# Two batches of v loaded without a cast, and two more TensorE transposes handed to the DMA, in a fused attention and MLP kernel

## The chip, the cores and the metric

One core of one Trainium2 chip runs the whole program. The metric is device time in microseconds (us). Engines are named as in the profile: PE (TensorE matmul), PEld (its weight load), DVE (VectorE), ACT (ScalarE), POOL (GpSimd), SP (SyncE, which here only issues DMAs).

## The reference

Attention with a relative position bias, eight batches of eight heads, 576 positions, head size 64; then a two-layer MLP with a leaky ReLU on all 4608 tokens. Inputs and output are float32; the kernel computes in bfloat16 with float32 accumulation.

```python
q, k, v: (8, 8, 576, 64)     bias_table: (32, 8)
scores = scale * q @ k.T + bias[bucket(|i - j|)]     # scale = 1/8
attn = softmax(scores);  a = attn @ v                # (8, 8, 576, 64)
x = a.transpose(0, 2, 1, 3).reshape(4608, 512)
h = x @ w_in                                         # (512, 2048)
out = maximum(0.01 * h, h) @ w_out                   # (2048, 512)
```

## The kernel before, in words

**The unit of work** is a pair of heads: `items` lists 32 pairs, n = 0 to 31, four to a batch (`n_pairs` = 4, `b` the batch, `p` the pair in it). For each pair, q and k are turned so that the head size lies on the partitions (`transpose_q`, `transpose_k`, lines 287 to 295), scores are made key by query (`qk_mm`, 297), exponentiated on ACT (`exp`, 322), multiplied by the bias band on DVE (`band`, 334), and multiplied with v (`av_tails`, 352, for the last 64 keys; `av`, 365, for the other 512, once for each head of the pair). `av` ends with a reciprocal and a multiply on DVE (375, 376) into `opair`, bf16. `x_transposes` (382) turns `opair` into `xT`, the MLP's input.

**Two ways to turn.** With TensorE: 12 small transposes for q and 12 for k into PSUM (line 275), five for an output (394), each followed by a copy out of PSUM. By DMA: for q and k, `pair_rows` (252) first copies both heads side by side with two DVE copies (257), then `turn_by_dma` (263) issues one transposing DMA on SP's queue into a tile `tu`, and the copies of lines 290 and 294 read `tu`; for an output, one transposing DMA straight into `xT` (387). `by_dma(n)` (260) sends q and k of pairs n > 8 by DMA, and `x_by_dma(n)` (379) the outputs of n = 6, 8, 9 and on to 30. `turn_ahead` (637) prepares pair n + 2 in pass n for the first few pairs, n + 3 later. Where pair n + 1 goes by DMA, `begin(n)` (632) does this at the start of the pass; otherwise it is done in the loop behind the first `band` (line 734).

**Loads.** All of q, k, v and the weights come over GpSimd's DMA queue (q0 in the profile), which turns float32 into bf16 on the way. q, k and v have two buffers each (`qn`, `kn`, `vn`, `v4`; batch b uses buffer b % 2). GpSimd works its instructions off in order, a load that must wait holds up those behind it, and by the trace it issues a load only when the eighth load before it has landed. `loads(n)` (607) says what is issued in which pass: in pass 0 the first half of `w_in`, all of batch 1's v (four chunks of 128 positions, `load_v_part`, 117, and the 64 that are left, `load_v_tail`, 130), the second half of `w_in`, the first of `w_out`; in pass 2 half of batch 2's q and k and the rest of `w_out`; from batch 1 on, in passes p = 1, 2, 3, the next batch's loads, behind a one-element copy `tick` (621) that waits for an earlier pair's output.

**The MLP** is cut in pieces of four matmuls (`ffn_in`, 411, one of 16 column blocks for a block T of 512 tokens; `ffn_out`, 438). They are woven between the attention's steps by a plan (`plan`, `slot`, `moe_block`), in an order written out by hand; T = 0 begins in pass 4, T = 1 in pass 9. The activated values lie in `gt`, 16 KB a partition, from a pool with two buffers.

**Order of the loop pass** (714 to 782): loads and turning ahead; scores 0 and 1; `av_tails` and first `av` of pair n - 1; then, when pair n + 1 goes by DMA, `band(n, 0)` before `transpose_q(n + 1)`, otherwise after it; an MLP piece; second `av`; `band(n, 1)`; `transpose_k(n + 1)`; an MLP piece; scores 2, 3 and 4; `x_transposes(n - 1)`; the rest. Score 4 (line 305) writes the two PSUM banks that `av`'s outputs held, so it waits for DVE's second multiply.

Of the kernel before, what the change touches and what calls it, by code (L numbers as in the profile page):

```python
# [10 lines left out]
FP32 = mybir.dt.float32  # L11
BF16 = mybir.dt.bfloat16
# [25 lines left out]
def kernel(  # L38
# [10 lines left out]
    nc = tc.nc  # L49

    B, H, S, D = q.shape
# [4 lines left out]
    P = 128  # L56
    n_pairs = H // 2
    NJ = S // P
# [3 lines left out]
    TT = 512  # L62
    n_tt = NT // TT
    n_fc = DF // P
# [11 lines left out]
    gt_pool = ctx.enter_context(tc.tile_pool(name="gt", bufs=2))  # L76
# [17 lines left out]
    NBUF = 2  # L94
# [4 lines left out]
    vn = [per.tile([P, NJ, H, D + 1], BF16, name=f"vn{i}") for i in range(NBUF)]  # L99
# [9 lines left out]
    def load_qk(b, h0, h1):  # L109
        i = b % NBUF  # L110
        for src, dst in ((q, qn[i]), (k, kn[i])):
            nc.gpsimd.dma_start(  # L112
                out=dst[0:RQ, h0:h1, :, :].rearrange("r h c d -> r h (c d)"),
                in_=src[b, h0:h1, :, :].rearrange("h (r c) d -> r h (c d)", c=NC),
            )

    def load_v_part(b, chunks, h0=0, h1=H):
        for c in chunks:
            nc.gpsimd.dma_start(  # L119
                out=vn[b % NBUF][:, c, h0:h1, 0:D],  # L120
                in_=v[b, h0:h1, c * P : (c + 1) * P, :].rearrange("h s d -> s h d"),
            )

    def load_v_head(b, h):
        nc.gpsimd.dma_start(
            out=vn[b % NBUF][:, :, h, 0:D],
            in_=v[b, h, 0 : NJ * P, :].rearrange("(c s) d -> s c d", s=P),
        )

    def load_v_tail(b):  # L130
        for e in range(2):
            nc.gpsimd.dma_start(
                out=v4[b % NBUF][e * SL : (e + 1) * SL, :, 0:D],
                in_=v[b, e::2, NJ * P : S, :].rearrange("h s d -> s h d"),
            )
# [43 lines left out]
    for j, (u, lo, w, m) in enumerate(groups):  # L179
        copy = nc.scalar.copy if j % 3 == 2 else nc.vector.tensor_copy  # L180
        copy(out=ub[:, C0 + lo : C0 + lo + m * w].rearrange("h (m w) -> h m w", w=w),
             in_=e8[:, u : u + m].unsqueeze(2).to_broadcast([H, m, w]))
    row = ub[:, :]
    nc.vector.tensor_copy(
        out=ub[:, C0 - BAND + 1 : C0],
        in_=bass.AP(tensor=row.tensor, offset=row.offset + C0 + BAND - 1,
                    ap=[list(row.ap[0]), [-1, BAND - 1]]),
# [32 lines left out]
    load_qk(0, 4, 6)  # L220
    clear_edges(nc.vector, 1)
    load_v_head(0, 0)
    load_v_head(0, 1)
    load_v_tail(0)
    load_qk(0, 6, H)
# [7 lines left out]
    def load_w_in(half):  # L233
        o = slice(half * (DF // 2), (half + 1) * (DF // 2))
        nc.gpsimd.dma_start(out=w_in_sb[:, :, o], in_=moe_w_in[:, o].rearrange("(c p) f -> p c f", p=P))

    def load_w_out(half):
        n = n_fc // 2
        nc.gpsimd.dma_start(
            out=w_out_sb[:, half * n : (half + 1) * n, :],  # L240
            in_=moe_w_out[half * n * P : (half + 1) * n * P, :].rearrange("(f p) e -> p f e", p=P),
        )
# [4 lines left out]
    N = len(items)  # L247
# [10 lines left out]
                                  in_=src[b % NBUF][0:RQ, 2 * p : 2 * p + 2, :, :].rearrange("r e c d -> r c e d"))  # L258

    def by_dma(n):  # L260
        return n > 2 * n_pairs

    def turn_by_dma(n):
        t = turned[n] = tu_pool.tile([P, 2 * NC, RQ], BF16, name="tu")
# [2 lines left out]
    def turned_pair(n, j):  # L267

        if by_dma(n):
            return turned[n][:, j * NC : (j + 1) * NC, :].rearrange("p c r -> p r c")  # L270
        ps = ps_m_pool.tile([P, 8 * P], BF16, name="ps_t", tag="m")
        b, p = items[n]
        for c in range(NC):
            for e in range(2):
                nc.tensor.transpose(ps[e * D : (e + 1) * D, c * RQ : (c + 1) * RQ],  # L275
                                    in_=(qn, kn)[j][b % NBUF][0:RQ, 2 * p + e, c, :],
                                    identity=ident[0:RQ, 0:RQ])
        return ps[:, 0:S].rearrange("p (c r) -> p r c", c=NC)
# [98 lines left out]
                                in1=rcp.to_broadcast([P, NJ + 1, D]), op=ALU.mult)  # L377

    def x_by_dma(n):
        return n_pairs + 2 <= n < N - 1 and n != 2 * n_pairs - 1  # L380

    def x_transposes(n):
        b, p = items[n]
        opair = ops_[n]
        w = (NJ + 1) * P
        if x_by_dma(n):
            nc.sync.dma_start_transpose(
                out=xT[p][:, b * S : b * S + w].rearrange("p (i t) -> p i t", t=P),
                in_=opair.rearrange("p i d -> p (i d)"),
            )  # L390
            return
        ps = ps_m_pool.tile([P, 8 * P], BF16, name="ps_tx", tag="m")
        for ic in range(NJ + 1):
            nc.tensor.transpose(ps[:, ic * P : (ic + 1) * P], in_=opair[:, ic, :], identity=ident)  # L394
        nc.vector.tensor_copy(out=xT[p][:, b * S : (b + 1) * S], in_=ps[:, 0:S])


    gts = {}
    rest = {"on": False, "turn": 0}

    def bank(name):

        if rest["on"]:
            turn = rest["turn"] = (rest["turn"] + 1) % 6
            if turn % 3 == 0:
                return ps_o_pool.tile([P, 512], FP32, name=name, tag=f"o{turn // 3}")
            if turn % 3 == 1:
                return ps_s_pool.tile([P, 512], FP32, name=name, tag="ps_s")
        return ps_m_pool.tile([P, 512], FP32, name=name, tag="m")

    def ffn_in(T, f, spare=None):
        if f == 0:
            gts[T] = gt_pool.tile([P, n_fc, TT], BF16, name="gt")
        t0 = T * TT
        if spare is None:
            pm = bank("pm1")
        else:
            pm = ps_o_pool.tile([P, 512], FP32, name="pm1", tag=f"o{spare}")
        for c in range(n_cc):
            nc.tensor.matmul(pm, lhsT=w_in_sb[:, c, f * P : (f + 1) * P], rhs=xT[c][:, t0 : t0 + TT],  # L420
                             start=(c == 0), stop=(c == n_cc - 1))
        return pm
# [61 lines left out]
    def step(kind):  # L484
        T, s = made[kind], at_piece[kind]
        at_piece[kind] = (s + 1) % n_fc
        if at_piece[kind] == 0:
            made[kind] += 1
        return T, s
# [5 lines left out]
    def piece_in(spare=None):  # L495
        T, s = step("in")
        leaky(T, s, ffn_in(T, s, spare))
# [51 lines left out]
    def moe_block():  # L549

        done = 0
        while not can("out") and can("in") and done < 4 and room["left"] > 0:
            T, f = step("in")
            leaky(T, f, ffn_in(T, f, 0 if done == 3 and room["left"] > 1 else None), done == 1)
            room["left"] -= 1
            done += 1
            if done < 3:
                yield
        while done < 2:
            done += 1  # L560
            yield
        if room["split"]:
            yield
            piece_out()
            piece_out()
        elif can("out") and room["left"] >= 4:
            for part in range(4):
                piece_out()
                room["left"] -= 1
                if part == 1:  # L570
                    yield
            moe(2, 0 if room["left"] > 1 else None)
        else:
            yield
            moe(2)
        yield
# [30 lines left out]
    def loads(n):  # L607

        b, p = items[n]
        if n == 0:  # L610
            load_w_in(0)
            load_v_part(1, range(NJ))
            load_v_tail(1)
            load_w_in(1)
            load_w_out(0)
        elif n == 2:
            load_qk(2, 0, H // 2)
            load_w_out(1)
        if b < 1 or p < 1 or b > B - 2:
            return  # L620
        nc.gpsimd.tensor_copy(out=tick, in_=ops_[n - 2][0:1, 0, 0:1])  # L621
        if p == 1:
            load_qk(b + 1, H // 2, H)
            load_v_part(b + 1, (0,))
        elif p == 2:
            load_v_part(b + 1, (1, 2, 3))
        else:
            load_v_tail(b + 1)
            if b + 2 < B:
                load_qk(b + 2, 0, H // 2)  # L630

    def begin(n):
        loads(n)
        if by_dma(n + 1):
            turn_ahead(n)

    def turn_ahead(n):
        for m in range(n + 2, min(n + AHEAD + 1, N)):
            if by_dma(m) and m - (AHEAD if m > 2 * n_pairs + 2 else 2) == n:
                pair_rows(m)  # L640
                turn_by_dma(m)
# [47 lines left out]
    n = n_pairs  # L689
# [24 lines left out]
    for n in range(n_pairs + 1, N + 1):  # L714
        live = n < N
        more = n + 1 < N
        if x_by_dma(n - 2):
            finished(n - 2)
# [30 lines left out]
        if not x_by_dma(n - 1):  # L749
            finished(n - 1)  # L750
# [5 lines left out]
        if room["only"]:  # L756
            exp(n, 3, ps_b)
            moe(2)
            exp(n, 4, ps_c)
            score(n, 5)  # L760
            T, f = step("in")
            room["left"] -= 1

            def last_bands():
                band(n, 5)
                band(n, 4)

            leaky(T, f, ffn_in(T, f), True, last_bands)
            moe(room["left"])
            continue  # L770
# [44 lines left out]
```

## Time and profile before

| | |
|---|---|
| median of 3 runs | 377.47 us (377.23 to 381.31) |
| the profiled execution's own time | 378.04 us |
| its span, first to last instruction | 376.3 us |
| PE busy | 366.1 us, 97% of the span |
| PE, granted clock | 1.00 |
| GpSimd's DMA queue (q0) | 53696 packets, 47.2% of 16 engines' span |
| hardware queue (q1: SP's stores and transposes) | 50472 packets, 31.7% |
| v loads of 128 positions | 28 of 128 KB each (as bf16), 5.2 us to landing in the median |
| transposing DMAs for q and k / for outputs | 23, 4.0 us / 24, 4.3 us to landing in the median |

In a row of a timeline the columns are start, length (both us), engine, line, operation, output<-input, count, and in brackets the idle time before it with what ended it. "Landing" counts from issue to the last byte. A row of the DMA view gives packets, megabytes, and the time that the packets took, as a share of 16 engines; packets overlap, so it can be over 100%.

### The profile page before, as it was taken

The numbers are of one execution on the slowest core, as the hardware profiler recorded it, in microseconds if no ns is written. First come the engines' busy times: TensorE is split into PE (matmuls) and PEld (weight loads), VectorE is DVE, ScalarE is ACT, GpSimd is POOL, SyncE is SP. The second block draws the span as 40 slices with busy tenths as digits, with TensorE's granted clock in tenths as the row PEclk, the third lists the DMA queues.
The fourth block names the chain that finished last, engine by engine and source line by source line (L and its number), as shares of the span: only waits on it lengthen the run. The fifth ranks groups of instructions, "written<-read, shape, count | busy, mean of one in ns | idle before, by whom it ended". The sixth has DMA issues, their size and how long they took to land.

```text
span 376.3 us, 8737 instructions
## 1 busy us (share of the span) xinstructions
PE 366.1 (97%) x3604; PEld 186.7 (50%) x3604; DVE 199.1 (53%) x502; ACT 239.9 (64%) x376; POOL 77.3 (21%) x118
## 2 busy tenths in 40 slices
PE   7879999999999999999999999999999999999996
PEld 3455555554555555555545545555555544444442
DVE  3678577777657666666755666655553300200221
ACT  5998886568856787777866666767777255055000
POOL 8763422333023303330323033100000000000000
PEclk9999999999999999999999999999999999999999
DMA  8999999998599959997998399453111000110212
GB/s 104 189 194 186 206 199 120 181 179 121 77 119 157 145 85 123 151 152 91 142 118 132 72 124 127 74 79 77 47 47 47 28 30 0 59 54 0 82 60 84
DMA packets 104351, 40.06 MB, mean 106 GB/s; under 512 B 83184, under 2 KB 98808, under 8 KB 104312
## 3 DMA queue, kind: packets, MB, share of 16 engines
q0 software_dynamic: 53696, 18.36, 47.2%
q1 hardware_dynamic: 50472, 21.02, 31.7%
q8 instruction: 28, 0.46, 0.5%
q10 hardware_dynamic: 144, 0.13, 0.1%
q14 instruction: 11, 0.09, 0.1%
HBM read 37.68 MB, written 9.45 MB: 125 GB/s over the span
## 4 chain that ended last, share of the span: by engine, by line
PE 89%; DMA 5%; POOL 2%; DVE 2%; ACT 1%; issue 1%; DVEq 0%; ACTq 0%; POOLq 0%
PE pm L447 34%; PE pm L420 32%; PE ps_o L372 10%; PE ps_s L312 8%; DMA vn<-in_v_dram 3%; PE ps_s L315 2%; DMA v<-in_v_dram 1%; PE ps_o L361 1%; PE ps_q L305 1%; DVE opair L376 1%; PE ps_tx L394 1%; PE ps_t L275 1%; ACT at L325 1%; POOL kn L112 1%; POOL qn L112 0%
## 5 line engine op out<-in xcount | busy, mean ns | idle before, releaser
L420 PE MATMUL pm<-xT,w_in_sb 128*128 128x512 bf16 x576 | 138.4, 379 | 0.1
L433 ACT ACTIVATE gt<-pm 128x512 bf16<-128x512 f32 x138 | 82.5, 603 | 86.2 <-PE pm L420 85.7
L447 PE MATMUL pm<-w_out_sb,gt 128*128 128x512 bf16 x576 | 132.5, 379 | 0.0
L325 ACT ACTIVATE at<-ps_s 128x1024 bf16<-128x1024 f32 x128 | 124.2, 1028 | 8.2 <-PE ps_s L312 8.1
L348 DVE TENSOR_TENSOR at<-at,hk 128x768 bf16<-128x768 bf16 (+3 forms) x160 | 71.0, 453 | 32.7 <-ACT at L328 19.9
L447 PEld LDWEIGHTS <-gt 128*128 128x128 bf16 x576 | 53.0, 98 | 60.6
L420 PEld LDWEIGHTS <-w_in_sb 128*128 128x128 bf16 x576 | 52.0, 98 | 54.8 <-issue 0.7
L465 DVE COPY y<-pm 128x512 f32<-128x512 f32 x33 | 22.8, 691 | 76.6 <-PE pm L447 76.6
L372 PE MATMUL ps_o<-vn,at 128*128 128x65 bf16 x1280 | 49.8, 194 | 0.4 <-DMA vn<-in_v_dram 0.4
L372 PEld LDWEIGHTS <-at 128*128 128x128 bf16 x1280 | 44.7, 97 | 9.5 <-issue 1.2
L312 PE MATMUL ps_s<-qt,kt 64*128 64x512 bf16 x256 | 40.1, 381 | 3.5 <-ACT at L325 3.0
L375 DVE RECIPROCAL rcp<-ps_o 128x5 f32<-128x5 f32 x64 | 12.3, 192 | 45.1 <-PE ps_o L372 45.1
L376 DVE TENSOR_TENSOR opair<-ps_o,rcp 128x320 bf16<-128x320 f32 x64 | 31.5, 492 | 3.3
L119 POOL DMA_DIRECT2D vn<-in_v_dram x32 | 29.6, 931 | 10.0 <-PE ps_s L312 5.6
L621 POOL COPY tick<-opair 1x1 bf16<-1x1 bf16 x18 | 4.7, 263 | 130.8 <-DVE opair L376 130.8
L312 PEld LDWEIGHTS <-kt 64*128 64x128 bf16 x256 | 8.4, 94 | 29.0 <-issue 21.5
L332 ACT ACTIVATE at<-ps_s 128x576 bf16<-128x576 f32 x32 | 21.8, 681 | 0.2 <-PE ps_s L316 0.2
L328 ACT ACTIVATE at<-ps_q 128x256 bf16<-128x256 f32 x64 | 21.5, 402 | 0.3 <-PE ps_q L305 0.2
L457 ACT COPY y<-pm 128x256 f32<-128x256 f32 x1 | 0.4, 372 | 27.5 <-DVE y L457 27.5
L294 DVE COPY kt<-tu 128x576 bf16<-128x576 bf16 x23 | 15.5, 674 | 0.0
L290 DVE COPY qt<-tu 128x576 bf16<-128x576 bf16 x23 | 15.0, 650 | 0.4 <-DMA tu<-pr 0.4
L112 POOL DMA_DIRECT2D qn<-in_q_dram x18 | 14.1, 782 | 4.2 <-PE ps_t L275 1.3
(57 smaller groups left out, 175.0 us busy)
## 6 DMA issues: line engine op xcount, KB each, us to landing
out_dram<-y SPq DMA_DIRECT2D x35, 256.0 KB, 2.3
qn<-in_q_dram POOLq DMA_DIRECT2D x14, 288.0 KB, 5.9
kn<-in_k_dram POOLq DMA_DIRECT2D x14, 288.0 KB, 7.1
vn<-in_v_dram POOLq DMA_DIRECT2D x28, 128.0 KB, 5.2
w_in_sb<-in_moe_w_in_dram POOLq DMA_DIRECT2D x2, 1024.0 KB, 12.9
w_out_sb<-in_moe_w_out_dram POOLq DMA_DIRECT2D x2, 1024.0 KB, 15.9
qn<-in_q_dram POOLq DMA_DIRECT2D x4, 144.0 KB, 4.3
kn<-in_k_dram POOLq DMA_DIRECT2D x4, 144.0 KB, 4.6
```

The source lines that it names most:

```text
L119: nc.gpsimd.dma_start(out=vn[b % NBUF][:, c, h0:h1, 0:D], in_=v[b, h0:h1, c * P : (c + 1) * P, :].rearrange("h s d -> s h d"),)
L312: nc.tensor.matmul(ps[:, e, :], lhsT=kt[r, u * P : (u + 1) * P], rhs=qt[r, 0:512], start=True, stop=True)
L325: nc.scalar.activation(at[:, :, u, 0:512], ps, AF.Exp, scale=scale)
L328: nc.scalar.activation(at[:, e, :, 512:S], ps[e][:, 0 : NJ * SL].rearrange("p (c i) -> p c i", i=SL), AF.Exp, scale=scale)
L332: nc.scalar.activation(at4[:, 0:S], ps.rearrange("p e i -> p (e i)")[:, 0:S], AF.Exp, scale=scale)
L348: nc.vector.tensor_tensor(out=o, in0=o, in1=m, op=ALU.mult)
L372: nc.tensor.matmul(ps[:, ic, :], lhsT=at[:, o : o + P], rhs=vn[b % NBUF][:, c, 2 * p + e, :], start=False, stop=(ic == NJ and c == NJ - 1))
L376: nc.vector.tensor_tensor(out=opair[:, :, e * D : (e + 1) * D], in0=ps[:, :, 0:D], in1=rcp.to_broadcast([P, NJ + 1, D]), op=ALU.mult)
L420: nc.tensor.matmul(pm, lhsT=w_in_sb[:, c, f * P : (f + 1) * P], rhs=xT[c][:, t0 : t0 + TT], start=(c == 0), stop=(c == n_cc - 1))
L433: nc.scalar.activation(g, pm, AF.Prelu, bias=0.0, scale=1.0, alpha=0.01)
L447: nc.tensor.matmul(pm, lhsT=gt[:, f, ts * P : (ts + 1) * P], rhs=w_out_sb[:, f, :], start=(f == 0), stop=(f == n_fc - 1))
L465: nc.vector.tensor_copy(out=y, in_=pm)
```

## The change

Batches 1 and 2 of v are no longer cast by the DMA. Their chunks of 128 positions are loaded as float32, still over GpSimd's queue, into a tile `stage` that takes one of the two `gt` buffers, and four copies on GpSimd per batch cast them into `vn`. The casts for batch 1 stand in pass 2, ahead of the loads of batch 2's q and k; those for batch 2 in pass 7, ahead of the load of v's tail. The tails are loaded as before, and so is v from batch 3 on. The ninth pair (n = 8) has its q and k turned by DMA, prepared in pass 6, and the sixth pair's output (n = 5) goes by DMA in pass 6. By that, pass 7 turns pair 9 ahead at its start and runs `band(7, 0)` before `transpose_q(8)`.

```diff
+    stage = gt_pool.tile([P, 2 * NJ, H, D], FP32, name="stage", tag="gt")
+
+    def stage_v(b, chunks):
+        for c in chunks:
+            nc.gpsimd.dma_start(
+                out=stage[:, c, :, :],
+                in_=v[b, :, c * P : (c + 1) * P, :].rearrange("h s d -> s h d"),
+            )
+
+    def cast_v(b):
+        for c in range(NJ):
+            nc.gpsimd.tensor_copy(out=vn[b % NBUF][:, c, :, 0:D], in_=stage[:, c, :, :])

     def by_dma(n):
-        return n > 2 * n_pairs
+        return n > 2 * n_pairs - 1

     def x_by_dma(n):
-        return n_pairs + 2 <= n < N - 1 and n != 2 * n_pairs - 1
+        return n_pairs + 1 <= n < N - 1 and n != 2 * n_pairs - 1

         if f == 0:
-            gts[T] = gt_pool.tile([P, n_fc, TT], BF16, name="gt")
+            gts[T] = gt_pool.tile([P, n_fc, TT], BF16, name="gt", tag="gt")

         if n == 0:
             load_w_in(0)
-            load_v_part(1, range(NJ))
+            stage_v(1, range(NJ))
             load_v_tail(1)
             load_w_in(1)
             load_w_out(0)
         elif n == 2:
+            cast_v(1)
             load_qk(2, 0, H // 2)
             load_w_out(1)
...
+        load_v = stage_v if b == 1 else load_v_part
         if p == 1:
             load_qk(b + 1, H // 2, H)
-            load_v_part(b + 1, (0,))
+            load_v(b + 1, (0,))
         elif p == 2:
-            load_v_part(b + 1, (1, 2, 3))
+            load_v(b + 1, (1, 2, 3))
         else:
+            if b == 1:
+                cast_v(b + 1)
             load_v_tail(b + 1)
```

## The prediction

> **What bounds the kernel now.** I read the page first (busy times and slices), then busy time by stage, then the chain of waits in order of time, then the timelines of VectorE (DVE), GpSimd (POOL) and the SP queue between 26 and 82 us, where the change acts, and last the DMA queues microsecond by microsecond.
>
> ```profile
> PE 366.1 (97%) x3604; PEld 186.7 (50%) x3604; DVE 199.1 (53%) x502; ACT 239.9 (64%) x376; POOL 77.3 (21%) x118
> DMA  8999999998599959997998399453111000110212
> ```
> ```profile
> 47.75:56.44 8.69, 8.69 (x118) 5.04 (x118) 6.43 (x16) 7.15 (x11) 2.55 (x4) 1.00 1.46 198
> 56.44:65.68 9.24, 9.21 (x118) 5.08 (x118) 6.59 (x17) 6.55 (x10) 1.96 (x3) 1.00 2.20 122
> ```
>
> The second fence gives one row for each of the loop passes n = 6 and n = 7: start and end, length, then busy time of PE, PEld, DVE, ACT, POOL, the granted clock, DMA share, GB/s. TensorE is busy for 8.69 of 8.69 and 9.21 of 9.24 us, at full clock. So a removed PE instruction is a gain, and a wait put in front of PE is a loss of its full length: no later slack gives it back. The DMA line is the other half: from the second slice to the tenth the DMA engines are full too, and the change puts new transfers exactly there.
>
> **The change part by part.**
>
> *PE work removed, q and k of pair 8.* Chain of waits, pass n = 7 with its two groups of 12 transposes between the rows, against n = 9, which has none; the columns are start and length.
>
> ```profile
> 52.28 0.39 PE ps_tx L394 x5
> ...
> 57.20 0.71 PE ps_o L372 x20
> 58.28 0.97 PE pm L420 x4
> 59.25 0.61 PE ps_o L372 x20
> 60.23 0.97 PE pm L420 x4
> 61.74 0.12 PE ps_q L305 x8
> ```
> ```profile
> 76.65 0.71 PE ps_o L372 x20
> 77.36 0.86 PE pm L420 x4
> 78.22 0.61 PE ps_o L372 x20
> 78.84 0.86 PE pm L420 x4
> ```
>
> From the start of the first to the end of the last row it is 60.23 + 0.97 - 57.20 = 4.00 us with the transposes and 78.84 + 0.86 - 76.65 = 3.05 us without: 0.95 us saved. *The output of pair 5:* the five transposes of line 394 in pass n = 6 take 0.39 us, all saved. Their copy on DVE goes too; DVE is off the path there. Together -1.34 us, if nothing new waits.
>
> *Two copies added on DVE in pass n = 6.* `pair_rows(8)` now stands between `band(6, 0)` and the reciprocal of pair 5's second head. The same two copies in the same place in pass n = 7:
>
> ```profile
> 50.63 0.41 DVE L348 TENSOR_TENSOR at<-at,hk 128x512 bf16<-128x512 bf16 x1
> 51.44 0.49 DVE L376 TENSOR_TENSOR opair<-ps_o,rcp 128x320 bf16<-128x320 f32 x1
> ...
> 59.31 0.41 DVE L348 TENSOR_TENSOR at<-at,hk 128x512 bf16<-128x512 bf16 x1
> 59.65 0.35 DVE L257 COPY pr<-qn 96x768 bf16<-96x768 bf16 x1
> 60.18 0.18 DVE L375 RECIPROCAL rcp<-ps_o 128x5 f32<-128x5 f32 x1
> ...
> 68.97 0.66 DVE L290 COPY qt<-tu 128x576 bf16<-128x576 bf16 x1 [0.40 <-DMA tu<-pr]
> 69.54 0.19 DVE L375 RECIPROCAL rcp<-ps_o 128x5 f32<-128x5 f32 x1
> ```
>
> From the band to the reciprocal it is 60.18 - 59.31 = 0.87 us there, so in pass n = 6 the reciprocal starts at 50.63 + 0.87 = 51.50 and the multiply after it at about 51.7 instead of 51.44: 0.27 us later. Behind it waits the PE matmul group of line 305 (the ps_q scores use the banks that the multiply frees), which follows the multiply within 0.2 us. I charge half, 0.13 us (ends 0 and 0.27). The copy of k needs batch 2's k, loaded here:
>
> ```profile
> L112 POOL DMA_DIRECT2D kn<-in_k_dram x1: 673/673/673, 36.9 to 36.9; - x1
> ...
> DMA to landing us min/median/max: 14.1/14.1/14.1
> ```
>
> It lands at 36.9 + 14.1 = 51.0, and the copy would start at about 51.2: just in time. The casts now stand ahead of this load on GpSimd's queue and push its issue to about 39.4 (below), but two weight halves are still queued in front of it then, so I take the landing as unchanged.
>
> *The transpose of pair 8 by DMA.* This is the term that decides. SP can issue it about 0.4 us after the second copy starts (60.29 against 59.9 in pass n = 7), at 51.6.
>
> ```profile
> 60.29 2.13 SPq L265 DMA_TRANSPOSE tu<-pr  x1
> ```
> ```profile
> DMA to landing us min/median/max: 3.3/4.0/8.1
> ```
>
> The 8.1 us is this first one, pair 9's, the only one issued while loads were queued deep; the quiet ones take 4.0. How it got on (packets per stretch; the row of 1184 is a stretch with one such transpose, 93.8 to 97.5; the next rows are 63 to 64, and 64 to 65 with its q0; then q0 in 67 to 68, and q0 in 52 to 53):
>
> ```profile
> q1 hardware_dynamic: 1184, 0.30, 58.0%
> ...
> q1 hardware_dynamic: 28, 0.01, 3.4%
> ...
> q1 hardware_dynamic: 179, 0.05, 116.4%
> q0 software_dynamic: 162, 0.12, 94.1%
> ...
> q0 software_dynamic: 7, 0.00, 3.0%
> ...
> q0 software_dynamic: 245, 0.21, 128.9%
> ```
>
> Its first packets came 3.5 us after the issue, it moved some 180 packets per us while GpSimd's queue q0 still had work, and finished only because q0 ran dry at 67. At 51.6 q0 is full and stays so past 60. With 3.5 + 1184/180 = 10.1 us pair 8's transpose lands at 61.7. Ends: 4.0 us (55.6) and, at 28 to 179 packets per us mixed (about 100), 15.3 us (66.9). I take 61.7, since the q0 row for 52 to 53 is like the stretch with 179, not like the dry one.
>
> A rule of the Trainium skill bears on it: "DMA: Bandwidth & Descriptors", section on queues, rings and completion order, says that each DMA engine takes turns between its queues packet by packet. By the bare row, 8.1 us, the landing would be 59.7 and the sum -0.8 us; by the rule the transpose pays one packet of loads for each of its own, which is the longer figure. The trace agrees with the rule for 64 to 65: 179 packets of q1 beside 162 of q0.
>
> *Who waits for it.* In pass n = 7 the copy `transpose_q(8)` on DVE now waits for the landing; queued behind it on DVE are the reciprocal (0.57 us after the copy's start, 69.54 - 68.97), 0.19 us, and the multiply, 0.49 us: 1.25 us to free the banks of line 305. PE reaches line 305 at 61.74 - 0.95 - 0.39 + 0.13 = 60.53. So PE waits for landing + 1.25 - 60.53 = landing - 59.28: 2.4 us for 61.7. Ends 0 and 7.6.
>
> *SP and the later transposes.* Pair 5's output transpose follows on SP, pair 9's is issued some 2 us earlier than now; pair 9's copy is needed at 68.97 and had 0.40 us of wait. I charge nothing (cover: its earlier issue; 0.4 us either way).
>
> *The casts of batch 1.* They stand on GpSimd behind `load_w_out(0)`, and av of pair 4 needs all four.
>
> ```profile
> 2.68 0.23 POOL masks.py:197 MEMSET ident<- 128x128 bf16 x1
> 16.14 0.27 POOL L139 MEMSET vn<- 128x32 bf16 x1
> 34.16 0.89 POOL L239 DMA_DIRECT2D w_out_sb<-in_moe_w_out_dram  x1 [4.22 <-DMA w_in_sb<-in_moe_w_in_dram]
> ```
> ```profile
> L119 POOL DMA_DIRECT2D vn<-in_v_dram x1: 878/878/878, 26.6 to 26.6; - x1
> ...
> DMA to landing us min/median/max: 11.9/11.9/11.9
> ```
> ```profile
> 39.75 0.78 PE L372 MATMUL ps_o<-vn,at 128*128 128x65 bf16 x20
> ...
> 76.58 0.78 PE L372 MATMUL ps_o<-vn,at 128*128 128x65 bf16 x20
> ```
>
> No row shows a GpSimd cast. 512 elements are 4 x 128: at most 0.92 us from the first memset, and 16 x 0.27 = 4.3 us from the strided one. Rows of 64 in 65 are nearly the contiguous case: 0.9 us. The last chunk lands at 26.6 + 11.9 = 38.5, its cast ends at 39.4, PE asks at 39.75: nothing, but with only 0.35 us to spare. The load itself now writes 256 KB instead of 128 KB per chunk. No load here is uncast; the same bytes are read, so I take the same time (ends: 1 us less to 1 us more per chunk).
>
> *The casts of batch 2.* Before, its last chunk was issued at 50.1:
>
> ```profile
> L119 POOL DMA_DIRECT2D vn<-in_v_dram x1: 873/873/873, 50.1 to 50.1; - x1
> ...
> DMA to landing us min/median/max: 15.0/15.0/15.0
> ```
>
> It lands at 65.1; cast by 66 to 69; asked for at 76.58. Queued behind the casts on GpSimd are v's tail and half of batch 3's q and k, some 8 us later than now, needed by 76 to 77. I charge nothing; without the 7 us of cover it would be up to 1 us. The gt buffer is free long before TensorE's first product for it at 77.36.
>
> **Sum.** -0.95 - 0.39 + 0.13 + 2.4 = +1.2 us. Against the profiled execution (378.04 us, of which 376.3 are span) that is 379.2; its time lies 0.57 us over the median of the three runs, 377.47, so for the median I say 378.7.
>
> **Rivals.**
> 1. *The transpose is in time* (landing by 59.3). For it: 4.0 us is the median, and a faster uncast v would thin q0. Against: the first packets alone took 3.5 us under load. The sum is -1.2: 376.3.
> 2. *The transpose stays behind q0 until it drains*, landing 65 to 67, which decides from 64.3 on: there the wait reaches 5.0 us and the whole change +3.8. For it: the trace's only loaded case was let go by the drained queue, not before. Against: its 180 packets per us with q0 at work. At 66 the wait is 6.7, the sum +5.5: 383.0.
> 3. *GpSimd's casts are slow.* Four must fit between 35.05 (34.16 + 0.89) and 39.75, so from 1.2 us each PE waits; at 2.2 us they end at 43.9: 4.1 us more, 380.4 if pair 8's wait is gone by then, 382.8 with it. DVE is 74% busy (6.43 of 8.69) and its bands read two operands each. The Trainium skill, "SBUF — State Buffer", section "SBUF: two separate sides", says that GpSimd and a VectorE operation with two SBUF inputs lock each other out of a shared port for a whole instruction; no run here shows a case of it yet.
> 4. *Uncast v is slower by 1 us a chunk*: the fourth lands 4 us later, 42.5, is cast at 43.4, and PE waits 3.6 us; pair 8's load is late by as much, so the rest stands: +4.8, 382.3.
>
> **Chances.** Forecast 0.46, rival 1 0.25, rival 2 0.12, rival 3 0.10, rival 4 0.07. About 1% (3.8 us) is what a measurement of this kernel can tell from no change. Forecast and rival 1 stay within it; rivals 2 to 4 mostly pass it, 0.22 of their 0.29; faster by more than 1% needs more than every removed instruction gives: 0.02. The likeliest case's own range is 377.5 to 380.5; the range for 8 in 10 reaches from rival 1 at 376.0 to 383.0.
>
> **What would show it.** Right: a DVE wait of 1 to 4 us for the DMA of tu before the copy of line 290 in pass n = 7, and a PE wait for DVE's multiply at line 305 just after; no line 275 or 394 in the removed places; casts near 0.9 us that end before 39.75. Wrong: a landing of pair 8's transpose under 8 us; a PE wait at line 372 for a POOL copy near 40 us; a PE wait at line 361 near 76 us for v's tail, or a DVE wait at line 257 there for batch 3's k.

## The result and the profile after

The changed kernel takes 389.44 us (median of 4 runs, 387.72 to 391.19), the kernel before 377.6 (377.23 to 381.31, four runs by now): a ratio of 1.030, 95% interval [1.026, 1.034]. The prediction, 378.7 with 376.0 to 383.0, was wrong. The profiled execution took 391.19 us; its span is 389.4, against 376.3 before.

The page of the changed kernel; the second to fourth line cut the span in 40 slices of 9.7 us each:

```profile
PE 364.6 (94%) x3521; PEld 186.6 (48%) x3575; DVE 199.1 (51%) x503; ACT 239.9 (62%) x376; POOL 82.2 (21%) x126
...
PE   7889992599999999999999999999999999999996
...
PEclk9999997599999999999999999999999999999999
DMA  8999999989959995899699859955111100110122
```

TensorE's busy time is 1.5 us less than before (366.1), and it has a hole in the seventh and eighth slice. The granted clock falls there too. The loss has one place. Passes n = 6, 7 and 8 of the changed kernel, from the start of one pass's `av_tails` to the next (a line number of the kernel before is 13 higher now from `pair_rows` to `ffn_out`: 305 is 318, 290 is 303):

```profile
48.19:56.72 8.53, 8.28 (x112) 4.72 (x112) 6.50 (x18) 7.14 (x12) 1.38 (x3) 1.00 1.26 215
56.72:79.36 22.64, 10.81 (x94) 5.05 (x93) 6.08 (x17) 6.33 (x11) 5.26 (x8) 0.70 1.18 107
79.36:89.57 10.21, 10.16 (x107) 5.36 (x106) 6.94 (x19) 5.57 (x9) 2.63 (x4) 1.00 1.12 151
```

Before, the three took 8.69, 9.24 and 10.21 us. Pass 6 is 0.16 us shorter, pass 7 is 13.4 us longer, pass 8 is the same. The chain of waits through pass 7 (start, length):

```profile
51.03 0.53 DVE pr L270 x2
51.57 0.03 DVE rcp L388
51.60 19.25 DMA tu<-pr
70.85 0.02 issue
70.87 0.64 DVE qt L303
71.51 0.11 DVE rcp L388
71.63 0.02 issue
71.65 0.50 DVE opair L389
72.15 0.05 issue
72.20 0.39 PE ps_q L318 x7
```

Pair 8's transpose is issued at 51.60 and lands 19.25 us later. The copy of line 303 waits for it, the reciprocal and the multiply stand behind that copy on DVE, and score 4 on PE behind the multiply: the predicted chain, with a wait of another size. TensorE's timeline in pass 7, the kernel before first (line 305), then the changed one (line 318):

```profile
61.58 0.28 PE L305 MATMUL ps_q<-qt,kt 64*128 64x64 bf16 x8
61.89 1.89 PE L447 MATMUL pm<-w_out_sb,gt 128*128 128x512 bf16 x8
...
66.12 0.32 PE L361 MATMUL ps_o<-v,at 64*128 64x65 bf16 x10
```
```profile
60.45 0.19 PE L318 MATMUL ps_q<-qt,kt 64*128 64x64 bf16 x1
72.20 0.39 PE L318 MATMUL ps_q<-qt,kt 64*128 64x64 bf16 x7 [11.56 <-DVE opair L389]
72.52 3.60 PE L460 MATMUL pm<-w_out_sb,gt 128*128 128x512 bf16 x8
...
79.36 0.32 PE L374 MATMUL ps_o<-v,at 64*128 64x65 bf16 x10
```

That splits the 13.4 us. From the start of pass 7 to score 4 PE needs 60.45 - 56.72 = 3.73 us instead of 61.58 - 56.88 = 4.70: -0.97. It then waits 11.56. What is left after score 4 has begun is 79.36 - 60.45 - 11.56 = 7.35 us instead of 66.12 - 61.58 = 4.54: +2.81. Most of that, 1.71, is that the same eight matmuls of line 460 (447 before) take 3.60 us instead of 1.89. The clock from score 4 almost to the next pass was 0.59:

```profile
72.20:79.00 6.80, 6.58 (x26) 2.62 (x29) 2.32 (x6) 1.31 (x3) 0.22 (x1) 0.59 0.77 111
```

What the DMA queues moved meanwhile, microsecond 57 to 58 and then 65 to 66 (packets, MB, share of 16 engines; the GB/s row cuts the microsecond in 40 slices of 0.025 us, by the start of the packets):

```profile
DMA packets 132, 0.19 MB, mean 191 GB/s; under 512 B 78, under 2 KB 92, under 8 KB 132
...
q0 software_dynamic: 67, 0.17, 99.3%
q1 hardware_dynamic: 65, 0.02, 29.0%
```
```profile
GB/s 61 0 0 0 0 0 31 102 31 164 0 0 0 0 0 0 0 31 195 92 164 0 0 0 0 0 0 0 0 113 41 164 0 0 0 0 0 0 0 0
...
q1 hardware_dynamic: 68, 0.02, 141.7%
q0 software_dynamic: 3, 0.01, 4.8%
```

At 57 to 58 the transposes get about one packet for each of GpSimd's queue, but there are few turns: 65 in a microsecond, where the prediction had 180. Of q0's 67 packets 40 are over 2 KB (132 - 92), and they carry nearly all of its 0.17 MB, some 4 KB each. Not every microsecond is one for one (59 to 60: 210 of q1 to 48 of q0); over 56 to 68 q1 moved 1395 packets, 116 per us, for all the transposes in flight.

At 65 to 66 q0 moves only three packets, but it isn't done: GpSimd's casts at 66.87, 67.98 and 69.01 still wait for chunks of batch 2 to land. Three slices of the GB/s row, 0.27 us apart, show 164 GB/s, which is 4.1 KB in 0.025 us: one packet of q0 each. q1's packets start in a burst about each of them, 68 / 3 = 23 for one, and between the bursts nothing starts. A packet of q0 takes 4.8% x 16 / 3 = 0.26 us. So in this row the transposes advance by one burst for each 4 KB packet that is left, though the three together fill less than one of the 16 engines (4.8% x 16 = 0.77 us). The packets of q1 took 1.417 x 16 / 68 = 0.33 us each there, where the 1184 quiet ones of the prediction (58% of 16 engines over 3.7 us) took 0.029. Why so little of q0 holds up a whole transpose is not shown; the views don't tell the engines apart. Over the whole run q0 has 46016 packets instead of 53696: 960 fewer for each of the eight uncast chunks.

### The profile page after: what moved, and what is told of

Same layout as the page of the kernel before. It is cut to its first block, busy times and chain, and to the rows that moved or that the text cites. A ratio compares the mean times of both kernels' runs of the same rounds, so it can differ in the third digit from the quotient of the medians.

```text
span 389.4 us, 8637 instructions
## 1 busy us (share of the span) xinstructions
PE 364.6 (94%) x3521; PEld 186.6 (48%) x3575; DVE 199.1 (51%) x503; ACT 239.9 (62%) x376; POOL 82.2 (21%) x126
## 3 DMA queue, kind: packets, MB, share of 16 engines
q0 software_dynamic: 46016, 19.40, 42.7%
## 4 chain that ended last, share of the span: by engine, by line
PE 84%; DMA 5%; DVE 5%; ACT 3%; issue 1%; another core or an unknown queue 1%; DVEq 0%; ACTq 0%
PE pm L460 32%; PE pm L433 28%; PE ps_o L385 10%; PE ps_s L325 7%; DMA tu<-pr 5%; ACT at L338 2%; PE ps_s L328 1%; PE ps_o L374 1%; PE ps_w L612 1%; DVE at L361 1%; DVE opair L389 1%; PE ps_q L318 1%; DVE qt L303 1%; PE ps_tx L407 1%
## 5 line engine op out<-in xcount | busy, mean ns | idle before, releaser
L433 PE MATMUL pm<-xT,w_in_sb 128*128 128x512 bf16 x543 | 136.3, 379 | 2.1 <-DVE qt L303 0.2
L341 ACT ACTIVATE at<-ps_q 128x256 bf16<-128x256 f32 x64 | 21.5, 401 | 10.4 <-PE ps_q L318 10.3
L119 POOL DMA_DIRECT2D vn<-in_v_dram x24 | 22.2, 932 | 2.4 <-issue 1.1
L325 PEld LDWEIGHTS <-kt 64*128 64x128 bf16 x256 | 8.4, 94 | 29.0 <-issue 21.5
L318 PE MATMUL ps_q<-qt,kt 64*128 64x64 bf16 x256 | 9.6, 192 | 11.7 <-DVE opair L389 11.6
L318 PEld LDWEIGHTS <-kt 64*128 64x128 bf16 x256 | 7.8, 95 | 19.2 <-DVE opair L389 12.5
## 6 DMA issues: line engine op xcount, KB each, us to landing
w_in_sb<-in_moe_w_in_dram POOLq DMA_DIRECT2D x2, 1024.0 KB, 13.4
```

Of the source, the lines that this page charges most:

```text
L119: nc.gpsimd.dma_start(out=vn[b % NBUF][:, c, h0:h1, 0:D], in_=v[b, h0:h1, c * P : (c + 1) * P, :].rearrange("h s d -> s h d"),)
L325: nc.tensor.matmul(ps[:, e, :], lhsT=kt[r, u * P : (u + 1) * P], rhs=qt[r, 0:512], start=True, stop=True)
L341: nc.scalar.activation(at[:, e, :, 512:S], ps[e][:, 0 : NJ * SL].rearrange("p (c i) -> p c i", i=SL), AF.Exp, scale=scale)
```

## The experiments

In the table are the medians, the ratio to the kernel before run beside it on the same chip, the lengths of passes 7, 8 and 9, and from the issue of pair 8's transpose to the start of the copy that waits for it (a dash where that copy doesn't wait, or TensorE turns pair 8). The passes before the fourth differ by up to 2.8 us in sum between these profiles, so the lengths tell more than the spans.

| kernel | median us | ratio, 95% | pass 7 | 8 | 9 | transpose us |
|---|---|---|---|---|---|---|
| before | 377.4 to 378.2 | 1 | 9.24 | 10.21 | 9.07 | - |
| changed | 389.44 | 1.030 [1.026, 1.034] | 22.64 | 10.21 | 9.07 | 19.3 |
| E1 v cast by DMA | 381.98 | 1.009 [1.006, 1.011] | 11.03 | 11.16 | 10.87 | 10.4 |
| E2 output 5 on PE | 389.89 | 1.030 [1.027, 1.033] | 20.38 | 10.21 | 9.07 | 18.4 |
| E3 pair 8 on PE | 380.92 | 1.007 [1.004, 1.009] | 9.24 | 12.19 | 9.07 | - |
| E4 uncast v alone | 378.52 | 1.001 [0.998, 1.003] | 9.24 | 10.21 | 9.07 | - |
| E5 busy wait | 388.62 | 1.027 [1.025, 1.030] | 19.54 | 10.21 | 9.07 | 18.8 |
| E6 batch 1 uncast | 382.36 | 1.012 [1.008, 1.016] | 11.96 | 10.21 | 9.07 | 9.6 |
| E7 cast, copy later | 382.69 | 1.011 [1.008, 1.015] | 8.19 | 11.62 | 11.66 | 9.9 |
| E8 and loads later | 377.79 | 1.000 [0.998, 1.002] | 8.19 | 10.21 | 9.08 | - |
| E9 output 5 alone | 378.04 | 1.000 [0.998, 1.002] | 9.24 | 10.21 | 9.07 | - |
| E10 as E8, uncast | 377.46 | 0.997 [0.995, 0.999] | 8.19 | 10.22 | 9.06 | - |
| E11 as E8, spread | 376.67 | 0.996 [0.994, 0.997] | 8.19 | 10.21 | 9.07 | - |
| E12 padded tile | 389.04 | 1.028 [1.024, 1.032] | 18.88 | 10.21 | 9.07 | 15.4 |
| E13 two chunks uncast | 388.49 | 1.025 [1.021, 1.030] | 21.08 | 10.22 | 9.07 | 17.5 |
| E14 runs halved | 390.01 | 1.028 [1.023, 1.034] | 18.70 | 10.21 | 9.07 | 15.2 |
| E15 as E11, uncast | 377.01 | 0.997 [0.996, 0.999] | 8.19 | 10.21 | 9.07 | - |
| E16 changed again | 391.04 | 1.036 [1.034, 1.037] | 23.02 | 10.21 | 9.07 | 20.6 |
| E17 busy wait again | 387.38 | 1.027 [1.026, 1.028] | 19.05 | 10.21 | 9.07 | 18.4 |

One execution of E7 took 1080.99 us, for a reason that the record doesn't show; its row is of the other three.

**Which parts it takes: E1 to E4 and E6.** The change has three parts: v uncast, pair 8 by DMA, output 5 by DMA. E1 keeps the last two (against the changed kernel; `...` marks lines left out):

```diff
-            stage_v(1, range(NJ))
+            load_v_part(1, range(NJ))
...
-            cast_v(1)
...
-        load_v = stage_v if b == 1 else load_v_part
+        load_v = load_v_part
...
-            if b == 1:
-                cast_v(b + 1)
```

> The change without its first part: v of batches 1 and 2 is cast by the DMA as before, the ninth pair's q and k and the sixth output still go by DMA. Theory A (the transpose starves behind GpSimd's load queue, whatever it loads): pair 8's transpose still lands 14 to 19 us after its issue, the wait before line 305 is 7 to 11 us, 385 to 389 us. Theory B (the uncast loads travel in packets of 4 KB, 16 times fewer, and the transpose gets one turn per packet): with the cast loads' small packets it lands 8 to 11 us after its issue, the wait is 0.5 to 4 us, 377 to 381 us.

With cast loads the landing falls from 19.25 us to 10.35, and PE's wait from 11.56 to 2.64. E1, DVE in passes 7 to 9, then TensorE in pass 7, and its queues in 61 to 62:

```profile
63.04 0.64 DVE L290 COPY qt<-tu 128x576 bf16<-128x576 bf16 x1 [2.99 <-DMA tu<-pr]
...
73.92 0.65 DVE L290 COPY qt<-tu 128x576 bf16<-128x576 bf16 x1 [2.64 <-DMA tu<-pr]
...
84.20 0.65 DVE L290 COPY qt<-tu 128x576 bf16<-128x576 bf16 x1 [2.08 <-DMA tu<-pr]
```
```profile
64.37 0.29 PE L305 MATMUL ps_q<-qt,kt 64*128 64x64 bf16 x7 [2.64 <-DVE opair L376]
```
```profile
q1 hardware_dynamic: 385, 0.09, 83.8%
q0 software_dynamic: 375, 0.05, 77.8%
```

Again about one for one, but q0's packets have 0.05 MB / 375 = 0.13 KB now, and the transposes get 385 turns. The second and third wait are new: the transposes of pairs 9 and 10 are late as well, and passes 8 and 9 lose 0.95 and 1.80 us. With them the median, 381.98, is 1 us above theory B's range; landing and wait are within it. E2 to E4 take the parts away in turn, by the old bounds in `x_by_dma` and `by_dma`:

```diff
-        return n_pairs + 1 <= n < N - 1 and n != 2 * n_pairs - 1
+        return n_pairs + 2 <= n < N - 1 and n != 2 * n_pairs - 1
...
-        return n > 2 * n_pairs - 1
+        return n > 2 * n_pairs
```

E2 has the first, E3 the second, E4 both.

> The change with the sixth pair's output left on TensorE: one transpose fewer in SP's queue behind pair 8's. Theory C (the transposes hold each other up: xT and pair 9's tu were in flight together with pair 8's): pair 8's lands by 62 to 65, 380 to 384 us. Theories A and B: it lands at 69 to 71 all the same, 388 to 390 us.

> The change with the ninth pair's q and k left on TensorE: uncast v and the sixth output by DMA. If all the loss is the wait for pair 8's transpose (A, B, C alike): no wait of more than 1 us at line 305 in pass 7, full clock, 376.9 to 378. Theory D (uncast v costs by itself, through the casts on GpSimd or through v coming late): 380 us or more, with a PE wait at the av matmuls or DVE ones slowed beside the casts.

> Uncast v alone, both transposes left on TensorE. A, B, C: 377.3 to 378, within the noise of the kernel before, casts of 0.6 to 0.9 us ending before the av matmuls ask for them. D: over 380 us. Beside e3 it also prices the sixth output alone: 0.2 to 0.4 us.

E2: the output plays no part in the loss. E4: the uncast loads and casts by themselves cost nothing that the medians show (378.52, 0.5 us above the forecast; the kernel before beside it 378.06). E3 missed its forecast: with uncast v and output 5 by DMA, TensorE stands still in pass 8 in the middle of a group of line 385:

```profile
67.35 0.60 PE L385 MATMUL ps_o<-vn,at 128*128 128x65 bf16 x14
69.75 0.35 PE L385 MATMUL ps_o<-vn,at 128*128 128x65 bf16 x6 [1.81 <-issue]
```

"issue" means that nothing the profile shows held it; that cause stays open. (In 60 to 62 one 16 KB packet of the queue of instructions, q8, took 13.1% of 16 engines, 4.2 us, where the others of this profile took 0.9 to 1.8; it had ended at 65.7, so it is a lead and no proof.) So it is not a sum of parts: the uncast loads alone 0, with output 5 some 3 us, with pair 8 some 12. E6 asks which batch's loads it takes; it keeps `stage_v` and `cast_v` for batch 1 only:

```diff
-        load_v = stage_v if b == 1 else load_v_part
+        load_v = load_v_part
...
-            if b == 1:
-                cast_v(b + 1)
```

> The change with only batch 1's v uncast; batch 2's chunks, the ones in the queue beside pair 8's transpose, are cast by the DMA. Theory B (the packets of 4 KB beside the transpose): pair 8's transpose lands 9 to 12 us after its issue and the kernel is like the one with all of v cast, 380 to 383.5 us. Rival (batch 1's uncast load or its casts, which push half of batch 2's q and k back, are what delays it): 386 us or more.

E6 is like E1: it takes batch 2's chunks, which stand in the queue when pair 8's transpose is issued.

**What it is in the chunks: E12 to E14.** E12 puts a gap behind each head's row in `stage`:

```diff
-    stage = gt_pool.tile([P, 2 * NJ, H, D], FP32, name="stage", tag="gt")
+    stage = gt_pool.tile([P, NJ, H, 2 * D], FP32, name="stage", tag="gt")
...
-                out=stage[:, c, :, :],
+                out=stage[:, c, :, 0:D],
```

> The changed kernel with one edit: the float32 tile has a gap of 256 bytes behind each head's 256 bytes, so that a chunk's rows no longer lie side by side in SBUF. Bytes read, bytes written, issues and casts are the same. Theory A (the size of the packets): if the gap splits the 4 KB packets, q0 has up to 7680 packets more, pair 8's transpose lands in 10 to 13 us instead of 19, and the time is 381 to 384. Rival (the 256 KB written per chunk in place of 128, whatever the packets): landing 17 us or more, 388 to 391. If the gap leaves the packets at 4 KB, it tells nothing, and the time is that of the changed kernel.

E13 loads batch 2's chunks 0 and 1 with `stage_v` and 2 and 3 with `load_v_part`, and casts only the first two:

```diff
-            load_v(b + 1, (1, 2, 3))
+            if b == 1:
+                stage_v(b + 1, (1,))
+                load_v_part(b + 1, (2, 3))
+            else:
+                load_v_part(b + 1, (1, 2, 3))
```

> The changed kernel, with chunks 0 and 1 of batch 2's v uncast and chunks 2 and 3 cast by the DMA as before. Theory A (each uncast packet in the queue costs the transpose a turn that is longer): the landing of pair 8's transpose lies between 10.3 us (none uncast) and 19.25 us (four), near 15 us, and the time near 385.5 (383.5 to 387.5). Rival (only the depth of the queue at the end counts, so the two cast chunks behind decide): landing 10 to 12 us, 381.5 to 383. Rival 2 (one uncast chunk is enough): 18 us or more, 388 or more.

E14 loads each chunk of batch 2 in two halves of 32 values (w = 32, i = 0 and 1):

```diff
...
+                    out=stage[:, c, :, i * w : (i + 1) * w],
+                    in_=v[b, :, c * P : (c + 1) * P, i * w : (i + 1) * w].rearrange("h s d -> s h d"),
```

> The changed kernel, with each chunk of batch 2's v loaded in two halves of 32 of the 64 values: the same bytes in runs of 128 bytes instead of 256. Theory A (size of a packet): if 16 runs make a packet, q0 has 256 packets more, each of 2 KB, the transpose's turns come twice as often for the same bytes, and it lands in 13 to 17 us: 383 to 387. Rival (the bytes or the runs, not the packets): 19 us or more, 389 to 392. If the packets stay at 4 KB (q0 at 46016), it tells nothing of their size.

E12 left q0 at 46016 packets and E14 at 46080, so neither changed the size of the packets much, and by their own terms they tell nothing of it. That their transposes landed in 15.4 and 15.2 us, sooner than in the two profiles of the changed kernel (19.3 and 20.6), the runs don't explain. In E13 half of the chunks give 17.5 us, nearer to four (19.3) than halfway (14.8): over theory A's "near 15" and just short of rival 2's 18. Its median, 388.49, is over A's range and in rival 2's. E13's queues in 61 to 62:

```profile
q1 hardware_dynamic: 153, 0.04, 101.8%
q0 software_dynamic: 149, 0.06, 82.7%
```

One for one again, at 40% of E1's 385. That two uncast chunks suffice for most of the loss is shown; that it is the size of their packets is read from the rows, not shown by a run that changes only that.

**The clock: E5, E16, E17.** E5 and E17 are one kernel: 48 matmuls on unused data stand ahead of score 4 in pass 7, so that TensorE doesn't idle. E16 is the changed kernel, beside E17 on the same chip.

```diff
+            if n == 2 * n_pairs - 1:
+                pw = ps_m_pool.tile([P, 512], FP32, name="ps_w", tag="m")
+                for _ in range(48):
+                    nc.tensor.matmul(pw, lhsT=junk[:, 0:P], rhs=junk, start=True, stop=True)
+            ps_c = qk_mm(n, 4)
```

> The changed kernel with 48 junk matmuls (128x512, into a spare PSUM bank that nobody reads) put between the scores 3 and 4 of pass 7, where TensorE waits for pair 8's transpose; nothing else is changed. Theory E (some 2.8 us of the loss are the slower clock after 11.6 us of idle TensorE): the granted clock stays at 1.00 after the wait and the kernel comes to 386 to 387.5 us. Rival (the clock has nothing to do with the wait, or the wait alone is the whole loss): 389 to 391 us.

> The changed kernel itself, for the comparison with the next one on the same chip: 388 to 391, clock 0.98 to 0.987, pass 7 between 20 and 23 us by the landing of pair 8's transpose.

> The changed kernel with 48 matmuls on unused data ahead of score 4 of pass 7, so that TensorE doesn't idle in the wait. Theory A (the dropped clock costs 2 to 3 us of the loss): the median 2 us or more under that of the changed kernel beside it, clock 0.994 or more. Rival (the landing itself varies by some us and the clock costs less than 1 us of the median): within 1 us of it.

E5's profile had the clock back (0.999), but its median, 388.62, lay between its two forecasts. Side by side the busy wait takes 387.38 us (387.08 to 388.33) and the changed kernel 391.04 (390.42 to 391.84): work that computes nothing makes the kernel 3.7 us faster. From the start of the copy of line 303 to the next pass, E16 and then E17:

```profile
72.06:79.62 7.56, 5.89 (x29) 2.40 (x31) 4.44 (x10) 1.32 (x4) 3.10 (x5) 0.69 1.06 123
```
```profile
69.48:75.28 5.80, 5.70 (x37) 2.37 (x35) 3.95 (x10) 1.32 (x4) 1.55 (x3) 1.00 1.18 167
```

The clock makes up 1.8 us of this pair of profiles (2.7 in the first: 79.36 - 70.87 = 8.49). Of the 3.97 us between their passes 7 the rest is that E17's transpose landed 2.2 us sooner, which the runs don't explain.

**Can the transposes be had for nothing: E7 to E11, E15.** E7 has cast loads and moves pass 7's `transpose_q(8)` behind the second `av`, so that the multiply no longer stands behind the copy:

```diff
+        late = n == 2 * n_pairs - 1
-        if more:
+        if more and not late:
             transpose_q(n + 1)
...
+        if late:
+            transpose_q(n + 1)
         if more:
             transpose_k(n + 1)
```

> Cast v, both transposes by DMA, and in pass 7 the copy of pair 8's q on VectorE moved behind the second av's multiply and the band, next to k's. The transpose lands as late as before (9 to 12 us after its issue); if it costs only because the multiply for line 305 is queued behind the waiting copy, the 2.6 us wait at line 305 in pass 7 goes: 378 to 380 us, with the waits of passes 8 and 9 left. If the landing itself holds up PE (pair 8's scores), the wait moves to pass 8 and the time stays at 381 to 383.

Pass 7 shrinks to 8.19 us, the whole 1.05 gained, and passes 8 and 9 lose 1.41 and 2.59: the wait moved on to the next pairs' transposes. E8 thins the queue as well; to E7 it adds that batch 2's v, its tails and half of batch 3's q and k are loaded in pass 8 (and no longer in passes 5 to 7, by conditions left out here):

```diff
+        if n == 2 * n_pairs:
+            nc.gpsimd.tensor_copy(out=tick, in_=ops_[n - 2][0:1, 0, 0:1])
+            load_v_part(2, range(NJ))
+            load_v_tail(2)
+            load_qk(3, 0, H // 2)
```

> As the run with the copy moved, and batch 2's v and the first half of batch 3's q and k loaded in pass 8 (behind a tick on pair 6's output) and not in passes 5 to 7, so that GpSimd's queue is empty sooner beside the first DMA transposes. Theory (the later waits, in passes 8 and 9, are transposes held up by the same loads): pair 8's and 9's transposes land 6 to 10 us after their issue, no wait over 0.5 us at line 305, 376 to 378 us. Rival: batch 2's v comes too late for pass 9 and PE waits there: 379 or more.

The waits are gone from all three passes, and the time is that of the kernel before (1.000 [0.998, 1.002]). E9 has only the output of pair 5 by DMA: E1's edit and the second of the two bounds above. E10 is E8 with batches 1 and 2 of v uncast; in pass 8:

```diff
-            load_v_part(2, range(NJ))
+            stage_v(2, range(NJ))
             load_v_tail(2)
             load_qk(3, 0, H // 2)
+            cast_v(2)
```

E11 is E8 with the second half of batch 3's q and k and its first chunk of v moved from pass 9 (p = 1) to 10 (p = 2). E15 is E10 with that same edit:

```diff
         if p == 1:
-            load_qk(b + 1, H // 2, H)
+            if b != 2:
+                load_qk(b + 1, H // 2, H)
-            if b > 1:
+            if b > 2:
                 load_v(b + 1, (0,))
         elif p == 2:
+            if b == 2:
+                load_qk(b + 1, H // 2, H)
+                load_v(b + 1, (0,))
```

> v of batches 1 and 2 cast by the DMA as before, pair 8 turned by TensorE; only the output of pair 5 goes by DMA. Theory A (a hardware transpose hurts in this stretch only beside uncast chunks): 377.2 to 377.8, that is -0.4 us for the five transposes of line 394 and nothing else, and pass 8 at 10.2 us. Rival (a transposing DMA here slows the loads whatever their kind, as with uncast chunks, where the sum was +3.3): 379 or more, with a wait of TensorE for v or a longer pass 7 or 8.

> As the late-load kernel (pass 7's q copy moved behind the second av's multiply; batch 2's v, tails and half of batch 3's q and k loaded in pass 8), but batches 1 and 2 of v stay uncast, with GpSimd's casts behind those loads. Theory A (4 KB packets starve whatever transpose is issued beside them): pair 8's transpose lands in 4 to 5 us, but those of pairs 10 and 11, issued near 70 us beside the chunks, take 15 us or more, and passes 8 and 9 grow by 2 to 6 us in sum: 379 to 384. Rival (an uncast load is harmless once the queue isn't deep, since it drains sooner): 377 to 378.3, transposes of pairs 10 and 11 at 12 us or less.

> The late-load kernel with cast loads, and the second half of batch 3's q and k and the first chunk of its v moved from pass 9 to pass 10. If what kept the transposes of pairs 10 and 11 at 11.5 us was the load queue in pass 9, they now land in 9 us or less and no multiply waits for them: 376.3 to 377.3, the -1.3 us of the removed instructions in full. Rival (nothing waited there any more): the same as the late-load kernel within 0.4 us, 377.3 to 378.2. Against both: the later loads make batch 3 wait, over 378.5.

> Batches 1 and 2 of v uncast, batch 2's v, tails and half of batch 3's q and k loaded in pass 8, and the second half of batch 3's q and k and the first chunk of its v moved from pass 9 to pass 10, pass 7's q copy behind the second av's multiply. Theory A (an uncast load costs only the transpose that stands beside it, and brings nothing by itself): 376.3 to 377.2, equal to the kernel with cast loads in the same places (376.67). Rival (the uncast load drains sooner and that helps): under 376.2.

E9's median, 378.04, is 0.2 us above its forecast, and its interval holds both that forecast and no change; pass 6 is 8.46 us instead of 8.69. E10 missed too, but it doesn't refute the theory: its chunks of batch 2, issued from 58.8 to 61.9 into an emptied queue, land in 4.5 to 6.7 us, and the transposes of pairs 10 and 11, issued at 65.6 and 67.6, have no packet moved before 68. They hardly meet, and the transposes land in 8.0 and 11.8 us. So whether uncast chunks need the deep queue of 52 us to do their harm stays open. E11 is the best of all: its transposes of pairs 10 and 11 land in 6.9 to 8.1 us (E8: 11.5 to 12.7), and pass 7's copy on DVE stands behind other work without a wait:

```profile
60.28 0.55 DVE L348 TENSOR_TENSOR at<-at,hk 128x768 bf16<-128x768 bf16 x1
60.75 0.65 DVE L290 COPY qt<-tu 128x576 bf16<-128x576 bf16 x1
```

At 376.67 us (376.39 to 377.14) it beats the kernel before, beside it at 378.16, by 0.4% [0.3%, 0.6%]: what the removed PE instructions are worth. E15 is no faster than E11 (377.01, on another chip; the intervals of the ratios overlap), so uncasting v brings nothing of its own here.

## Why the prediction was wrong

*Right: what the removed instructions give.* -0.95 was predicted for the turns of pair 8, -0.97 up to score 4 was found; for pass 6, -0.39 + 0.13 = -0.26 was predicted, -0.16 found.

*Right: the casts.* 0.9 us each and an end at 39.4, before TensorE asks. The changed kernel's first and last for batch 1, and the first for batch 2:

```profile
33.66 0.61 POOL L141 CAST vn<-stage 128x512 bf16<-128x512 f32 x1 [1.15 <-DMA stage<-in_v_dram]
...
37.29 0.94 POOL L141 CAST vn<-stage 128x512 bf16<-128x512 f32 x1 [0.30 <-DMA stage<-in_v_dram]
```
```profile
65.76 0.61 POOL L141 CAST vn<-stage 128x512 bf16<-128x512 f32 x1 [15.41 <-DMA stage<-in_v_dram]
```

0.61 to 0.94 us, the last of batch 1 done at 38.2; av of pair 4 is not held up. Rivals 3 (slow casts) and 4 (slower chunks that hold up batch 1) did not occur; E4 is the plainest evidence. A small cost beside the casts was put at nothing: in pass 4, where they run, three of DVE's band multiplies take 1.76 us instead of 1.35, TensorE waits 0.24 us for DVE, and the pass takes 9.21 us instead of 8.81. Pass 4 is 8.81 us in all six profiles without casts and 8.85 to 9.59 in all with them. That fits the contact of GpSimd and DVE that rival 3 names, and is far below its price.

*Right: the mechanism.* The transpose is issued at 51.60 (predicted 51.6), the copy waits for it, and from its landing to the release of score 4 it is 72.20 - 70.85 = 1.35 us (predicted 1.25).

*Wrong: the size of the wait, by the pace of the transpose.* "No load here is uncast; the same bytes are read, so I take the same time" was taken to cover batch 2 too, and with it that q0 would leave the transpose 180 packets per us. For the loads that the trace showed, the estimate was good: E1, with those loads, has a landing of 10.35 us, predicted 10.1, and a wait of 2.64, predicted 2.4. With uncast chunks in the queue it is 19.25 and 11.56. The term was thus mis-sized by 9.2 us. The 3.5 us to the first packets held (they come between 55 and 56); the 1184 / 180 = 6.6 us from there to the landing became 15. Same bytes was the wrong measure. What counts is how many turns the transpose gets, and how long one is: 65 packets to 67 in the rows of 57 to 58. The Trainium skill, "DMA: Bandwidth & Descriptors", section on queues, rings and completion order, says that an engine drains one whole packet of a queue before it goes to the next; the rows of 57 to 58 and E1's of 61 to 62 agree with it. The prediction cited that rule, but didn't ask what a packet of the new loads would be. At 65 to 66 a turn of q1 is a burst of some 23 packets, and its pace is still the 0.27 us from one 4 KB packet to the next; why the few packets that q0 has left hold the whole transpose is open.

*Not priced: the clock.* The wait of 11.56 us brought +2.81 us behind it in the profile (1.8 to 2.7 by the stretch from copy to pass end, against E17). The prediction let a wait cost its own length. The Trainium skill, "TensorE: Matmul & The Clock Gate", Part 1, says that the clock is halved after an idle window of some 3.4 us and restored after as long a busy one; the rows with 0.59 and 0.69 behind the wait, and 1.00 with the busy wait, agree, though the return took longer here: 0.59 over 6.8 us, if the clock is either half or full, is 5.6 us at half.

*Charged at nothing, and nothing only by luck: the later transposes.* "I charge nothing" for SP and pair 9 on; E1 lost 0.95 and 1.80 us in passes 8 and 9, E7 1.41 and 2.59. The cover that was named, an issue of pair 9's transpose some 2 us earlier, came to 0.27 us (60.02 instead of 60.29), because the issue of pair 5's output stood on SP for 6.10 us before it. In the changed kernel the long wait of pass 7 gave those transposes time to land.

*The rivals.* Rival 2 (the transpose stays behind q0 until it drains) had the right place and side at a chance of 0.12, but its landing of 65 to 67 came from the old queue's drain, and its 383.0 is 6 us short. Only rival 1 asked what the uncast load does to the transpose beside it, and expected help ("would thin q0"). Otherwise the two parts were priced alone, and E1 to E4 show that the loss lies in the pair.

## What to carry to other kernels

Price a DMA by what its packets do to the other queues, not by its bytes alone: before a new kind of load and a transposing DMA are put into the same stretch, count the turns that the transpose will get beside a deep queue. A transpose moved off TensorE pays only if its landing under load is covered and no in-order engine has urgent work queued behind its consumer; E7 shows that moving the consumer alone shifts the wait, E8 that moving the loads as well removes it. To a wait of TensorE add the slower clock behind it.

## What the runs showed of the hardware that was not expected

- A packet of a transposing DMA took 0.029 us in a quiet stretch and 0.33 us in 65 to 66 of the changed kernel, where q0 moved three 4 KB packets. The transposes then advanced in bursts, one for each of those packets, 0.27 us apart. Why so few hold up a whole transpose is open.
- A long wait of TensorE costs more than its length: the same eight matmuls took 3.60 us behind the 11.56 us, 1.89 us before; filling the wait with useless matmuls made the kernel 3.7 us faster (391.04 to 387.38), of which the clock is some 1.8 in the profiles.
- Loading float32 without a cast is not slower alone (E4: ratio 1.001 [0.998, 1.003]), though it writes twice the bytes, and takes 960 packets fewer per chunk.
- Operations of DVE run longer beside GpSimd's casts: 1.76 us instead of 1.35 for three band multiplies.
